# The right forms' loads and stores on ScalarE's queue: a change in layer 0's second MLP pair

## The chip, the cores and the metric

The kernel runs on one core of a Trainium2 chip. The metric is the device time of one execution in microseconds (us). Three executions of the kernel before took 1452.15, 1454.65 and 1456.01 us; their median is 1454.65.

The core has engines with instruction streams of their own: TensorE (PE in the profile) multiplies matrices, VectorE (DVE) does elementwise work on two operands, ScalarE (ACT) casts, copies and evaluates functions, GpSimd (POOL) does a little work here, and SyncE (SP) only starts transfers (DMAs). Each engine takes its instructions in the order in which the program gives them; between engines, semaphores hold an instruction until what it needs is there.

## What is computed

Two layers, each a Fourier mixing (matrix products with DFT matrices along the sequence and along the hidden dimension), then a block with a spatial shift and an MLP. Cut to what matters:

```python
for layer in range(2):
    n = layernorm(x)
    a, b = n @ hid_re.T, n @ hid_im.T
    x = x + seq_re @ a - seq_im @ b
    z = layernorm(x)
    h = gelu(layernorm(z) @ w1)              # four column groups, shifted by +1, -1, +2, -2 rows
    z1 = z + shifted(h) @ w2
    x = x + z1 + gelu(layernorm(z1) @ w3) @ w4
```

The sequence has 2048 rows (S), the hidden dimension is 512 (D), the MLP's inner dimension 1376 (F). All is float32. TensorE takes a rounded kind of it, so each operand is split into a **high** part (ScalarE casts it) and a **low** part (VectorE subtracts the high part from the operand), and each product is three matmuls: high x high, high x low, low x high (`mm3`).

## The kernel before

Many products go through a form of fast matrix multiplication with seven products of half blocks instead of eight. For layer 1's Fourier mixing along the hidden dimension, the seven **right forms** of the hidden DFT matrices are made once, split into high and low, and kept in DRAM (`hsd`, seven tensors of two halves each, L65). They are made in layer 0, beside the second MLP pair, and that is where the change is.

**The MLP by pairs.** The rows are treated in two pairs of chunks (`for pair in range(n_pairs)`, L1258). In layer 0's second pair (`next_too`), after a first stretch of two w4 parts, five **passes** run (`for p in range(NF // 2)`). A pass has seven products of six matmuls each (`prod`) in the order b1, b6, b5, b2, b7, b4, b3, each into one of four PSUM banks taken in turn, and between b7 and b4 two w4 parts of twelve matmuls each (one in pass 0). ScalarE copies the first product (`copy u`), VectorE adds the others to it and to one another (seven additions a pass, into the `rest` tiles; L567 is the helper `add`), and ScalarE applies gelu and casts. A product can start only when the last addition that reads its bank's former content is done; the bank of b5 is read by two additions, the later of which is behind b7. A w4 load (`w4_load`, L943, 512 KB) is issued on SP behind every w4 part, a w3 load (`w3_load`, L958, 1792 KB) at the end of passes 0 to 2.

**The points.** Work that belongs to something else is given out in small steps: `bg` is a list of steps, and `one()` (L1116) runs the next. There are 26 points in the pair: points 0 and 1 in the first stretch, then in each pass one behind b5 (A), one behind gelu of b7's sum (B), one behind each w4 part (C, D), and one at the end (E). Pass 0 has points 2 to 5, pass 1 points 6 to 10, pass 2 points 11 to 15, pass 3 points 16 to 20, pass 4 points 21 to 25. The list's own steps (`early`, L1133) prepare layer 1: for each of four row groups statistics, normalisation, sums, casts and lows, one step each.

**The right forms beside them.** They are made in four quarters, and each part is put around one of the list's steps. A quarter loads two row blocks, m (imaginary) and r (real), each 256 KB; their left and right halves are b11, b12, b21, b22. Four **sums** on VectorE make three sums in three buffers (numbered 0, 1, 2) and the last one over b12. Then four **parts** cast and split seven forms into these three buffers by turns: a cast of each on ScalarE ahead of the step, its low on VectorE behind the step, and, right behind the low, a store of 256 KB on SP (`highs_`, `lows_`, L1219 to 1232). So a quarter takes five points: the sums at the first, then the parts with 3, 2, 1 and 1 forms. Quarter n has points 5n to 5n + 4; the next quarter's m and r are loaded on SP behind its last two points, and the next sums come one point later. Quarter 0's m and r are loaded in pair 0 (`then[9]`, L1376).

On SP everything is in one row: the stores of the forms, which wait for their lows; m and r; the w4 and w3 loads. Buffers 1 and 2 lie where later gelu's output of the fifth pass is kept (`hx`, L126).

Of the kernel before, what the change touches and what calls it, by code (L numbers as in the profile page):

```python
# [8 lines left out]
F32 = mybir.dt.float32  # L9
F32R = mybir.dt.float32r  # L10
AF = mybir.ActivationFunctionType
ALU = mybir.AluOpType
# [33 lines left out]
def spectral_mlp_kernel(ctx: ExitStack, tc: tile.TileContext, x, ws, hs, w1, w2, w34, out):  # L46
    nc = tc.nc
# [17 lines left out]
    hsd = [[dram.tile([P, 2, CH], F32, name=f"hsd{i}{j}") for j in range(2)] for i in range(7)]  # L65
# [15 lines left out]
    base = -(-nc.sbuf_base // 32) * 32  # L81
# [76 lines left out]
    def piece(src, a=0, b=2):  # L158
        pieces.append((src, a, b))
        return len(pieces) - 1  # L160
# [25 lines left out]
    for layer in range(LAYERS):  # L186
        for c in range(NC):
# [15 lines left out]
            for k in range(NP):  # L203
# [4 lines left out]
                p = piece(ws[c, k][:, 2:4])  # L208
# [18 lines left out]
    raws, slots, sums, place = {}, {}, {}, {}  # L227
# [299 lines left out]
    def low(tf):  # L527
        nc.vector.tensor_tensor(tf[0][:, :, 1], tf[1][:, :, 1], tf[0][:, :, 0].bitcast(F32), op=ALU.subtract)
# [37 lines left out]
    def add(o, a, b, op=ALU.add):  # L566
        nc.vector.tensor_tensor(o, a, b, op=op)  # L567
# [290 lines left out]
    def by_pairs(layer, zs, xin, dst):  # L858
# [51 lines left out]
        def sum_of(*names):  # L910
            return lambda: b_sum(*names)
# [41 lines left out]
        def w3_load(n):  # L953
            if n >= n_pairs * (NF // 2):
                return
            if layer or n >= NF // 2:
                i = (n + (last_of(layer) and n >= NF // 2)) % 2
                nc.sync.dma_start(w3b[i].bitcast(F32), w3d[n % (NF // 2)])  # L958
                return
            nc.sync.dma_start(staged.rearrange("p f k w -> p f (k w)"), w34[2 * n : 2 * n + 2, :, 0].rearrange("f p w -> p f w"))  # L960
# [116 lines left out]
        steps = [(shifted, 0, g) for g in GORDER]  # L1077
# [32 lines left out]
        bg, prep = [], {}  # L1110
# [9 lines left out]
        def do_all(*fs_):  # L1120
            return lambda: [f() for f in fs_]
# [22 lines left out]
        def next_steps():  # L1144

            steps = (
                ((ay_lows, 2), (ay_sums, 3), (ay_highs, 3), (more, 1)),
                ((ay_lows, 3),),
                ((xp_stats, 4), (keep_rows, 8)),
                ((xp_stats, 5), (more, 2)),  # L1150
                ((xp_norm, 4),),
                ((xp_sums, 4), (xp_highs, 4), (more, 3)),
                ((ax_lows, 4), (xp_norm, 5)),
                ((ay_lows, 4), (ax_sums, 5), (ax_highs, 5), (more, 4)),
                ((ax_lows, 5), (keep_rows, 10)),
                ((ahead, 1), (more, len(pieces))),
                ((ahead, 1),),
                ((ahead, 1),),
                (),
            )  # L1160
            return [[do(*s)] for s in steps]
# [30 lines left out]
            ]  # L1192

        def hs_forms():
            steps = []
            for n in range(4):
                d, v = n // 2, slice(n % 2, n % 2 + 1)
                m, r = (at(f"hs{i}{n}", RAWS + (1 + i) * CH, 1, CH, dtype=F32) for i in range(2))
                fp = [both(f"hp{i}{n}", word, 1, 2, DH) for i, word in enumerate((RAWS + 3 * CH, STG, STG + CH))]
                steps += hs_quarter(m, r, fp, [(t[d][:, v], hs[(1, d)][:, v], hs[(0, d)][:, v]) for t in hsd])  # L1200
            return steps

        def hs_quarter(m, r, fp, places):
            b11, b12, b21, b22 = (t[:, :, v] for t in (m, r) for v in (left, right))
            raw = [tf[:, :, 1] for _, tf in fp]

            def load_m():
                nc.sync.dma_start(m, places[0][1])

            def load_r():  # L1210
                nc.sync.dma_start(r, places[0][2])

            def sums():
                add(raw[1], b12, b11, ALU.subtract)
                add(raw[2], b22, b12, ALU.subtract)
                add(raw[0], b22, raw[1], ALU.subtract)
                add(b12, raw[0], b21, ALU.subtract)

            def outs(*which):  # L1219
                which = [(i, n, raw[i] if src is None else src) for i, n, src in which]  # L1220

                def highs_():
                    for i, _, src in which:
                        act(fp[i][0][:, :, 0], src)

                def lows_():
                    for i, n, src in which:
                        t = fp[i][0]
                        nc.vector.tensor_tensor(t[:, :, 1], src, t[:, :, 0].bitcast(F32), op=ALU.subtract)
                        nc.sync.dma_start(places[n][0].rearrange("p i (l w) -> p i l w", l=2), t.bitcast(F32))  # L1230

                return highs_, lows_

            nothing = lambda: None
            parts = [
                (nothing, sums),
                outs((1, 3, None), (2, 4, None), (0, 2, None)),
                outs((1, 0, b11), (2, 1, b12)),
                outs((0, 6, b21)),
                outs((1, 5, b22)),  # L1240
            ]
            return [(load_m, load_r), *parts]

        def next_block(c, half, to):
            return lambda: b_in(c, half, to)
# [12 lines left out]
        for pair in range(n_pairs):  # L1258
# [10 lines left out]
            if next_too:  # L1269
                hcs[8:] = [hx[:, 0], hx[:, 1], rest[0]]  # L1270
                bg += [lows("t4"), *early]
                for n in range(4):
                    parts = work[6 * n + 1 : 6 * n + 6]
                    for i, (before, behind) in enumerate(parts):
                        more_ = []
                        if n < 3 and i > 2:
                            more_.append(work[6 * n + 6][i - 3])
                        bg[5 * n + i] = do_all(before, bg[5 * n + i], behind, *more_)
            elif pair:
                bg.append(lows("t4"))  # L1280
            sets = [rest[4:8], rest[4:8]]
# [6 lines left out]
            for i, names in enumerate((("11", "21"), ("12", "22"))):  # L1288
                for d in range(KD):
                    b = blk[names[d // 2]]  # L1290
                    v = slice(d * P, (d + 1) * P)
# [29 lines left out]
            for p in range(NF // 2):  # L1321
                prep = {} if kept else w_prep(p)
                u, v, x, y = sets[p % 2]
                w = w3b[(5 * pair + p) % 2]
# [48 lines left out]
            then = [[] for _ in range(NF + 2)]  # L1373
            if pair == 0:
                work = hs_forms()
                then[9] = [*work[0]]  # L1376
                next_blocks((3, 1, "22"))
                then[1] = [lambda: w3_load(NF // 2)]
                then[2] = [lambda: rows(xs[0], dst, 0, 2, False)]
                then[3] = [lambda: rows(xs[1], dst, 2, 2, False)]  # L1380
                then[4] = [sum_of("t1", "12", "11"), sum_of("t2", "22", "t1")]
                then[5] = [sum_of("t3", "22", "12"), sum_of("t4", "21", "t2"), highs("11", "21")]
                names = "11", "21", "12", "22", "t2", "t1", "t3", "t4"
                for i in range(6):
                    then[6 + i] += [lows(names[i]), highs(names[i + 2])]
                then[8] += [lambda: w3_load(NF // 2 + 1)]
                then[12] = [lows("t3")]
            if next_too:
                then = next_steps()
            if next_too:  # L1390
# [497 lines left out]
    for layer in range(LAYERS):  # L1888
# [4 lines left out]
        for c in range(NC):  # L1893
            if layer == 0 and c == 0:
# [22 lines left out]
                def second_low(i):  # L1917
# [165 lines left out]
        for i, (ri, dp) in enumerate(HORDER):  # L2083
# [76 lines left out]
```

## Time and profile before

| | us |
|---|---|
| median of three executions | 1454.65 |
| profiled execution | 1454.98 |
| its span in the profile | 1452.9 |
| TensorE busy | 1420.9 |
| VectorE busy | 1204.9 |
| ScalarE busy | 731.8 |
| the stretch with the five passes, in the span | 615.6 to 698.3 |

A row of the timeline gives the start, the duration, the engine, the line, the operation, the output and inputs, their sizes, and in brackets how long the engine stood idle ahead of it and what ended that. Names are those of the program with numbers left out: `hp` is a buffer of the forms, `hs` is m or r (and, in `hs<-in_hs`, their load), `hsd<-hp` a store, `rest` the tiles of the additions, `psa` to `psd` PSUM banks, `w3b` and `w4r` the weights. A name such as `hp11f` is buffer 1 of quarter 1. L1208 is the load of m, L1211 that of r, L1224 a cast, L1229 a low, L1230 a store. SPq is SP's queue: the time in it is that in which an issue occupies the queue. Rows that follow one another on VectorE and ScalarE overlap a little (0.42 us long, 0.34 us from start to start), so work that follows on is counted from start to start.

### The profile page before, as it was taken

What the parts mean: (1) busy time and instruction counts of PE and PEld (TensorE: products, weight loads), DVE (VectorE), ACT (ScalarE), POOL (GpSimd) and SP (SyncE); (2) the same over time, 40 slices, a digit from 0 to 9 for tenths busy, and PEclk for the clock granted to TensorE, in tenths of its full rate; (3) what the DMA queues carried; (4) which work ended last, traced back from release to release, by engine and by line L of the source; (5) the groups of instructions that cost most, each with busy time, mean ns of one, the idle gap of its engine ahead of it and who ended that gap; (6) DMA issues with size and microseconds to landing.
All of it is one profiled execution on the core that took longest, in us unless ns stands there. A gap on an engine that the chain in (4) does not pass through costs nothing.

```text
span 1452.9 us, 18506 instructions
## 1 busy us (share of the span) xinstructions
PE 1420.9 (98%) x6681; PEld 1188.4 (82%) x6681; DVE 1204.9 (83%) x1725; ACT 731.8 (50%) x1020; POOL 76.6 (5%) x105
## 2 busy tenths in 40 slices
PE   9999999999999999998999989989989999999999
PEld 7888888888888888876888878878878888899887
DVE  7986998989978897667799878879879797897676
ACT  5663554445566654344555443444445666444342
POOL 2100000000002000000000000000000011000000
PEclk9999999999999999999999999999999999999999
DMA  7867657568645758877655577576687537586864
GB/s 247 274 204 234 200 173 261 173 200 296 226 133 161 268 214 282 329 251 263 232 173 190 203 256 225 187 269 222 207 294 240 173 102 275 165 250 217 320 205 163
DMA packets 145628, 325.24 MB, mean 224 GB/s; under 512 B 10624, under 2 KB 61568, under 8 KB 142848
## 3 DMA queue, kind: packets, MB, share of 16 engines
q1 hardware_dynamic: 145536, 324.05, 66.9%
q8 instruction: 53, 0.87, 0.2%
q14 instruction: 39, 0.32, 0.1%
HBM read 262.41 MB, written 61.60 MB: 223 GB/s over the span
## 4 chain that ended last, share of the span: by engine, by line
PE 83%; DVE 9%; DMA 4%; ACT 2%; issue 2%; SPq 0%; DVEq 0%; ACTq 0%
PE psd L343 8%; PE psd L345 8%; PE psd L344 8%; PE psa L343 7%; PE psa L344 7%; PE psa L345 7%; PE psb L344 6%; PE psb L343 6%; PE psb L345 6%; PE psc L344 6%; PE psc L345 6%; PE psc L343 6%; DVE ring L300 1%; DVE rest L567 1%; DMA raw<-in_ws 1%
## 5 line engine op out<-in xcount | busy, mean ns | idle before, releaser
L300 DVE TENSOR_TENSOR ring<-raw,ring 128x1024 fp32r<-128x1024 f32 x102 | 124.2, 1220 | 19.0 <-ACT ring L279 18.7
L279 ACT CAST ring<-raw 128x1024 fp32r<-128x1024 f32 x103 | 107.8, 1051 | 56.3 <-PE psd L345 25.6
L383 POOL TENSOR_TENSOR rs<-ve,mhalf 128x4 f32<-128x4 f32 x16 | 25.0, 1562 | 746.1 <-DVE nm L382 746.1
L343 PE MATMUL psd<-ring,ay 128*128 128x512 f32 x126 | 50.1, 398 | 7.8 <-DVE tmp L567 7.8
L300 DVE TENSOR_TENSOR ring<-ring1f,ring 128x512 fp32r<-128x512 f32 (+1 forms) x56 | 53.3, 952 | 2.9 <-ACT ring L282 2.9
L286 ACT CAST ring<-ring0f 128x1024 fp32r<-128x1024 f32 x28 | 29.5, 1053 | 50.5 <-DVE ring0f L285 50.2
L286 ACT CAST ring<-ring2f 128x1024 fp32r<-128x1024 f32 x28 | 29.6, 1056 | 48.8 <-DVE ring2f L285 48.8
L343 PE MATMUL psd<-rawr,hf 128*128 128x256 f32 x168 | 47.7, 284 | 5.8 <-issue 4.8
L343 PE MATMUL psc<-ring,ay 128*128 128x512 f32 x128 | 50.2, 392 | 2.0 <-ACT rr11f L608 1.7
L300 DVE TENSOR_TENSOR ring<-ring3f,ring 128x1024 fp32r<-128x1024 f32 (+1 forms) x50 | 49.3, 986 | 3.0 <-ACT ring L282 2.6
L362 POOL TENSOR_TENSOR rs<-ve,mhalf 128x2 f32<-128x2 f32 (+2 forms) x33 | 29.2, 886 | 426.6 <-DVE nb L361 407.6
L391 ACT ACTIVATE tmp<-xs,nb,rs 128x512 f32<-128x512 f32 x56 | 43.3, 810 | 15.8 <-POOL nb L363 12.6
L344 PE MATMUL psb<-ring,ay 128*128 128x512 f32 x128 | 50.3, 393 | 0.8 <-DVE ring L300 0.8
L343 PE MATMUL psb<-ring,ay 128*128 128x512 f32 x128 | 50.5, 394 | 0.0
L345 PE MATMUL psb<-ring,ay 128*128 128x512 f32 x128 | 50.1, 391 | 0.0
L345 PE MATMUL psd<-ring,ay 128*128 128x512 f32 x126 | 49.9, 396 | 0.0
L344 PE MATMUL psc<-ring,ay 128*128 128x512 f32 x128 | 49.8, 389 | 0.0
L345 PE MATMUL psc<-ring,ay 128*128 128x512 f32 x128 | 49.8, 389 | 0.0
L344 PE MATMUL psd<-ring,ay 128*128 128x512 f32 x126 | 49.8, 395 | 0.0
L344 PE MATMUL psa<-ring,ay 128*128 128x512 f32 x126 | 49.0, 389 | 0.0
L343 PE MATMUL psa<-ring,ay 128*128 128x512 f32 x126 | 49.0, 389 | 0.0
L345 PE MATMUL psa<-ring,ay 128*128 128x512 f32 x126 | 49.0, 389 | 0.0
(896 smaller groups left out, 4757.8 us busy)
## 6 DMA issues: line engine op xcount, KB each, us to landing
raw<-in_ws SPq DMA_DIRECT2D x183, 512.0 KB, 5.2
w4r<-w4d SPq DMA_DIRECT2D x44, 512.0 KB, 5.3
rawr<-hsd SPq DMA_DIRECT2D x42, 512.0 KB, 4.8
w3b<-w3d SPq DMA_DIRECT2D x10, 1792.0 KB, 9.3
raw<-in_hs SPq DMA_DIRECT2D x32, 512.0 KB, 4.0
w3d<-w3b SPq DMA_DIRECT2D x5, 1792.0 KB, 7.0
hsd<-hp SPq DMA_DIRECT2D x28, 256.0 KB, 2.4
x1d<-tmp SPq DMA_DIRECT2D x12, 512.0 KB, 7.4
```

The costliest lines, as they stand in the source:

```text
L279: nc.scalar.copy(dest[:, a:b, 0], r[0][:, a:b])
L286: nc.scalar.copy(dest[:, :, 0], lo)
L300: nc.vector.tensor_tensor(lo, src, hi.bitcast(F32), op=ALU.subtract)
L343: nc.tensor.matmul(o, lh, rh, start=first, stop=False, skip_group_check=more)
L344: nc.tensor.matmul(o, lh, rl, start=False, stop=False, skip_group_check=more)
L345: nc.tensor.matmul(o, ll, rh, start=False, stop=last, skip_group_check=more)
L362: nc.gpsimd.tensor_tensor(rs[:, :n], ve[:, :n], mhalf[:, 0, :n], op=ALU.pow)
L383: nc.gpsimd.tensor_tensor(rs, ve, mhalf[:, :, :2], op=ALU.pow)
L391: nc.scalar.activation(o, s, AF.Identity, bias=mr[2], scale=mr[1])
L567: nc.vector.tensor_tensor(o, a, b, op=op)
```

## The change

The stores, and the loads of quarters 1 to 3, go through ScalarE's queue (`nc.scalar.dma_start`) instead of SP's. A store is no longer issued behind its low, but at the next point, ahead of everything else there. Quarter 0's loads stay on SP.

A quarter takes six points (`base = 6 * n - 1`): the sums at `base`, then five parts at the next five points with 2, 1, 2, 1 and 1 forms. Stores come at `base + 2` to `base + 6`. The m load is two points ahead of the sums, the r load in the sums' own point, ahead of the step; at that point first the last store of the quarter before, then the r load, then the step, then the sums. Quarter 0's sums move into pair 0 (`then[12]`), behind its last w4 part and ahead of the drain of its second chunk. The sums are reordered so that each buffer is overwritten in another turn: the forms are the same.

```diff
-            def load_m():
-                nc.sync.dma_start(m, places[0][1])
-
-            def load_r():
-                nc.sync.dma_start(r, places[0][2])
+            def load_m(queue=nc.scalar):
+                queue.dma_start(m, places[0][1])
+
+            def load_r(queue=nc.scalar):
+                queue.dma_start(r, places[0][2])
 
             def sums():
-                add(raw[1], b12, b11, ALU.subtract)
                 add(raw[2], b22, b12, ALU.subtract)
-                add(raw[0], b22, raw[1], ALU.subtract)
-                add(b12, raw[0], b21, ALU.subtract)
+                add(raw[1], raw[2], b11, ALU.add)
+                add(raw[0], b12, b11, ALU.subtract)
+                add(b12, raw[1], b21, ALU.subtract)
...
-                def lows_():
+                def rest_of():
                     for i, n, src in which:
                         t = fp[i][0]
                         nc.vector.tensor_tensor(t[:, :, 1], src, t[:, :, 0].bitcast(F32), op=ALU.subtract)
-                        nc.sync.dma_start(places[n][0].rearrange("p i (l w) -> p i l w", l=2), t.bitcast(F32))
+
+                def store():
+                    for i, n, _ in which:
+                        nc.scalar.dma_start(places[n][0].rearrange("p i (l w) -> p i l w", l=2), fp[i][0].bitcast(F32))
...
             parts = [
-                (nothing, sums),
-                outs((1, 3, None), (2, 4, None), (0, 2, None)),
-                outs((1, 0, b11), (2, 1, b12)),
-                outs((0, 6, b21)),
-                outs((1, 5, b22)),
+                outs((0, 3, None), (2, 4, None)),
+                outs((1, 2, None)),
+                outs((0, 0, b11), (2, 1, b12)),
+                outs((1, 6, b21)),
+                outs((0, 5, b22)),
             ]
...
+                ahead_, behind_ = [[] for _ in bg], [[] for _ in bg]
                 for n in range(4):
-                    parts = work[6 * n + 1 : 6 * n + 6]
-                    for i, (before, behind) in enumerate(parts):
-                        more_ = []
-                        if n < 3 and i > 2:
-                            more_.append(work[6 * n + 6][i - 3])
-                        bg[5 * n + i] = do_all(before, bg[5 * n + i], behind, *more_)
+                    load_m, load_r, sums_, parts = work[n]
+                    base = 6 * n - 1
+                    if n:
+                        ahead_[base - 2].append(load_m)
+                        ahead_[base].append(load_r)
+                        behind_[base].append(sums_)
+                    for i, (cast, rest_of, store) in enumerate(parts):
+                        ahead_[base + 1 + i].append(cast)
+                        behind_[base + 1 + i].append(rest_of)
+                        ahead_[base + 2 + i].insert(0, store)
+                bg[:] = [do_all(*a, f, *b) for a, f, b in zip(ahead_, bg, behind_)]
...
-                then[9] = [*work[0]]
+                then[9] = [lambda: (work[0][0](nc.sync), work[0][1](nc.sync))]
...
-                then[12] = [lows("t3")]
+                then[12] = [lows("t3"), lambda: work[0][2]()]
```

More of the change, by code (lines that the diff above doesn't have):

```diff
@@ L1194, in hs_forms @@
         def hs_forms():
-            steps = []
+            groups = []
             for n in range(4):
@@ L1199, in hs_forms @@
                 fp = [both(f"hp{i}{n}", word, 1, 2, DH) for i, word in enumerate((RAWS + 3 * CH, STG, STG + CH))]
-                steps += hs_quarter(m, r, fp, [(t[d][:, v], hs[(1, d)][:, v], hs[(0, d)][:, v]) for t in hsd])
-            return steps
+                groups.append(hs_quarter(m, r, fp, [(t[d][:, v], hs[(1, d)][:, v], hs[(0, d)][:, v]) for t in hsd]))
+            return groups
         def hs_quarter(m, r, fp, places):
@@ L1205, in hs_quarter, with cast @@
             raw = [tf[:, :, 1] for _, tf in fp]
-            def load_m():
-                nc.sync.dma_start(m, places[0][1])
-            def load_r():
-                nc.sync.dma_start(r, places[0][2])
+            def load_m(queue=nc.scalar):
+                queue.dma_start(m, places[0][1])
+            def load_r(queue=nc.scalar):
+                queue.dma_start(r, places[0][2])
             def sums():
-                add(raw[1], b12, b11, ALU.subtract)
                 add(raw[2], b22, b12, ALU.subtract)
-                add(raw[0], b22, raw[1], ALU.subtract)
-                add(b12, raw[0], b21, ALU.subtract)
+                add(raw[1], raw[2], b11, ALU.add)
+                add(raw[0], b12, b11, ALU.subtract)
+                add(b12, raw[1], b21, ALU.subtract)
             def outs(*which):
                 which = [(i, n, raw[i] if src is None else src) for i, n, src in which]
-                def highs_():
+                def cast():
                     for i, _, src in which:
                         act(fp[i][0][:, :, 0], src)
-                def lows_():
+                def rest_of():
                     for i, n, src in which:
@@ L1229, in lows_ @@
                         nc.vector.tensor_tensor(t[:, :, 1], src, t[:, :, 0].bitcast(F32), op=ALU.subtract)
-                        nc.sync.dma_start(places[n][0].rearrange("p i (l w) -> p i l w", l=2), t.bitcast(F32))
-                return highs_, lows_
-            nothing = lambda: None
+                def store():
+                    for i, n, _ in which:
+                        nc.scalar.dma_start(places[n][0].rearrange("p i (l w) -> p i l w", l=2), fp[i][0].bitcast(F32))
+                return cast, rest_of, store
             parts = [
-                (nothing, sums),
-                outs((1, 3, None), (2, 4, None), (0, 2, None)),
-                outs((1, 0, b11), (2, 1, b12)),
-                outs((0, 6, b21)),
-                outs((1, 5, b22)),
+                outs((0, 3, None), (2, 4, None)),
[3 more added lines that the diff above has]
+                outs((0, 5, b22)),
             ]
-            return [(load_m, load_r), *parts]
+            return load_m, load_r, sums, parts
         def next_block(c, half, to):
```

## The prediction

> **What bounds the kernel now.** I read the page first, then the busy time by stretches of 10 us, then who waits for whom while layer 0's second MLP pair runs its five passes, then the chain of waits and the queues one by one.
>
> ```profile
> span 1452.9 us, 18506 instructions
> PE 1420.9 (98%) x6681; PEld 1188.4 (82%) x6681; DVE 1204.9 (83%) x1725; ACT 731.8 (50%) x1020; POOL 76.6 (5%) x105
> ```
> ```profile
> 650.00:660.00 10.00, 8.42 (x38) 6.63 (x36) 6.05 (x17) 1.02 (x3) 1.00 (x2) 1.00 0.82 329
> 660.00:670.00 10.00, 7.88 (x33) 6.22 (x34) 7.21 (x14) 7.57 (x14) 0.00 (x0) 1.00 0.74 232
> ...
> 680.00:690.00 10.00, 9.67 (x36) 7.85 (x37) 7.88 (x16) 7.18 (x14) 0.00 (x0) 0.83 0.63 209
> ```
> ```profile
> PE psa L343 <- DVE rest L567: 4.3, 3, 3.1
> PE psd L343 <- DVE rest L567: 3.3, 2, 2.7
> ```
>
> TensorE sets the time: 98% busy over the whole. In the stretches (columns: length, then PE, PEld, DVE, ACT, POOL busy, the granted clock, DMA) it falls short here, and in the whole stage it waits for nothing but VectorE, 4.3 + 3.3 = 7.6 us, always for an addition that reads a PSUM bank. How much the stage loses in all comes from TensorE's own order in time.
>
> ```profile
> 615.57 0.39 PE L343 MATMUL psa<-b,w3b 128*128 128x512 f32 x1
> ...
> 643.72 0.40 PE L343 MATMUL psd<-b,w3b 128*128 128x512 f32 x1
> ...
> 661.48 0.50 PE L343 MATMUL psa<-b,w3b 128*128 128x512 f32 x1 [3.05 <-DVE rest L567]
> ...
> 662.97 0.39 PE L343 MATMUL psa<-b,w3b 128*128 128x512 f32 x1
> ...
> 680.33 0.79 PE L343 MATMUL psd<-b,w3b 128*128 128x512 f32 x1 [2.67 <-DVE rest L567]
> 680.93 0.63 PE L344 MATMUL psd<-b,w3b 128*128 128x512 f32 x1
> ...
> 690.18 0.39 PE L343 MATMUL psc<-w4r,h 128*128 128x512 f32 x1
> ...
> 698.34 0.39 PE L343 MATMUL psc<-w4r,h 128*128 128x512 f32 x1
> ```
>
> Between 690.18 and 698.34 stand 36 matmuls (two w4 parts of 12, two products of 6): 0.2267 us from start to start. The five passes hold 54 + 4 x 66 = 318 matmuls, which would take 72.1 us. They take 698.34 - 615.57 = 82.8 us. **10.7 us** are lost; what the 7.6 us of waits don't hold is slow restarting (after the 2.67 us wait 0.60 and 0.43 us from start to start, and a granted clock of 0.83 in that row). Why is VectorE late?
>
> ```profile
> 634.74 0.43 DVE L567 TENSOR_TENSOR hp11f<-hs 128x256 f32<-128x256 f32 x1 [2.38 <-DMA hsd<-hp]
> ...
> 635.88 0.42 DVE L567 TENSOR_TENSOR hs<-hp01f,hs 128x256 f32<-128x256 f32 x1
> ...
> 643.16 0.76 DVE L1229 TENSOR_TENSOR hp<-hs,hp 128x256 fp32r<-128x256 f32 x2 [0.99 <-ACT hp L1224]
> ...
> 653.82 0.43 DVE L567 TENSOR_TENSOR hp12f<-hs 128x256 f32<-128x256 f32 x1 [3.72 <-DMA hsd<-hp]
> ...
> 672.60 0.42 DVE L567 TENSOR_TENSOR hp13f<-hs 128x256 f32<-128x256 f32 x1 [3.25 <-DMA hsd<-hp]
> ```
> ```profile
> 646.66 0.42 SPq L1208 DMA_DIRECT2D hs<-in_hs  x1
> 647.18 0.38 SPq L943 DMA_DIRECT2D w4r<-w4d  x1
> 647.65 0.39 SPq L1230 DMA_DIRECT2D hsd<-hp  x1
> 648.09 0.47 SPq L1211 DMA_DIRECT2D hs<-in_hs  x1
> 648.66 0.44 SPq L958 DMA_DIRECT2D w3b<-w3d  x1
> ```
> ```profile
> 629.65 4.66 DMA hsd<-hp
> ...
> 648.09 6.22 DMA hs<-in_hs
> ```
>
> At each of the three later quarters VectorE stands still ahead of the first sum: 2.38, 3.72 and 3.25 us. That sum overwrites a buffer whose store was issued on SP just before (647.65), between a w4 load, the r load (648.09) and a w3 load; in the chain such a store lands after 4.66 us, the r load after 6.22. VectorE's lateness reaches TensorE some products later.
>
> **The change part by part.** *Work taken away:* none. Sums, casts, lows, 28 stores and 8 loads are as many as before; the sums only change their order and which buffer takes which. What moves is when, and on which queue.
>
> ```profile
> L1230 SPq DMA_DIRECT2D hsd<-hp x28: 319/357/411, 619.7 to 685.3; - x28
> ...
> DMA to landing us min/median/max: 2.0/2.4/6.0
> ```
> ```profile
> L1208 SPq DMA_DIRECT2D hs<-in_hs x4: 423/428/440, 599.8 to 665.9; - x4
> ...
> DMA to landing us min/median/max: 3.3/5.4/6.3
> ```
> ```profile
> SPq L1230 <- DVE hp L1229: 57.5, 17, 9.4
> ```
> ```profile
> 608.29 0.69 DVE L1108 TENSOR_TENSOR xs<-psc,xs 128x512 f32<-128x512 f32 x1 [3.12 <-PE psc L345]
> ```
>
> *SP* loses 28 stores and 6 loads, and with them 57.5 us of standing behind lows. TensorE shows no wait for a DMA in this stage, so its w4 and w3 loads coming earlier are worth nothing by themselves.
>
> *The first quarter's sums* move ahead of pair 0's drain. Four sums take 1.6 us (634.74 to 636.30). VectorE idles 3.12 us ahead of the drain at 608.29, and both loads were issued by 600.8, so with the longest landing of 6.3 us the sums run from 607.1 at the latest and delay the drain by at most 0.4 us; the drained banks are written first at 622.4. I take 0; if that cover failed, 1.6 us.
>
> *Six points a quarter* instead of five: VectorE has 6.05 + 7.21 = 13.3 us of work in the 20 us from 650, so 12.8 in the pass of 19.25 us from 643.72 to 662.97. The forms are 4 sums and 7 lows of about 0.34, 3.7 us; a sixth less in each pass leaves 12.2. A pass of 66 matmuls is 15.0 us.
>
> ```profile
> DVE hp L1229 <- ACT hp L1224: 4.5, 5, 1.4
> ...
> DVE h L766 <- ACT h L776: 3.0, 4, 0.8
> ...
> DVE ax2f L422 <- ACT xs L391: 0.4, 1, 0.4
> ```
>
> VectorE's waits for ScalarE's casts, (4.5 + 3.0) / 4 + 0.4 = 2.3 us a pass, stay. So it has 15.0 - 12.2 - 2.3 = 0.5 us to spare in each pass.
>
> *34 issues on ScalarE's queue.* No row of before shows one there. Lower bound 0, if they are hidden entirely; above, SP's row, 0.36 a store and 0.43 a load. I take SP's: 34 over 24 points and five points a pass are 7, 2.8 us beside ScalarE's 1.02 + 7.57 = 8.6, 11.4 of 15.0. What is queued behind a waiting store are the next cast, and then gelu and the copies that free PSUM banks.
>
> *The three sums that waited* now wait for the r load, issued ahead in the same point, right behind the store of the quarter's last part. Both can go out when the last low is done, if ScalarE's queue gets there in time. What the landing is on a queue of its own is unknown: 3.3 at least by the row, 6.3 at most; I take 4.0, nearer the least, because only its own store of 256 KB is ahead of it and no load of w4.
>
> ```profile
> 636.82 1.28 DVE L357 BATCH_NORM_STATS2 st<-xs 128x6 f32<-128x512 f32 x2
> ...
> 668.40 0.95 DVE L448 TENSOR_TENSOR ax<-ax2f,ax 128x768 fp32r<-128x768 f32 x1
> ```
>
> The durations are those from start to start in such rows (an addition 0.60, the statistics 1.75 with the small aggregations behind them, sums and lows 0.34).
>
> - Quarter 1 (point 5): pass 0's fifth product ends 30 matmuls after 615.57, at 622.4; from there two additions 1.2, ax sums 0.95, a low, low1 0.61, the last low and the ends between them give 626.1; store 0.4; the r load lands at 626.5 + 4.0 = 630.5. VectorE itself gets there at 630.0 (low2 behind gelu and cast, then ax lows 0.87). Wait 0.5. The addition that frees the bank came 5.9 us after the sums and comes 5.5 after them now, at 637.6; TensorE wants the bank 114 matmuls after 615.57, at 641.4. Nothing reaches it.
> - Quarter 2 (point 11): from the last low, VectorE has one addition and the statistics, 2.35 us; the load needs 0.36 + 4.0. Wait 2.0, of which 0.5 is to spare: 1.5 reaches TensorE.
> - Quarter 3 (point 17): four additions, 2.4 us. Wait 2.0, of which 1.5 reaches TensorE.
>
> Loss 3.0 instead of 10.7: a gain of 7.7 us. The profiled execution took 1454.98 us (its span of 1452.9 and 2.1 around it), 0.3 over the median of the three runs. 1454.98 - 7.7 = **1447.3 us**. With a landing of 3.3 both waits are 1.3, the loss 1.6, the time 1445.9; with 6.3 both are 4.3, the loss 7.6, the time 1451.9.
>
> That ScalarE's queue gets there in time means that a DMA doesn't stand behind a gelu that waits for VectorE. The Trainium skill, "Perfetto Trace Analysis", sections "DVE / Act Engine Instruction" and "DMA Instruction — HWDGE (DVE, Sync)", says that an ACT instruction is pushed into a wait queue and the sequencer goes on, while a DMA's own semaphore wait holds the sequencer. By the first half the sum above stands; by the second half all that follows a waiting store is held too. No run here shows either, since before has no DMA on that engine.
>
> **The rivals.**
>
> *A, the transfers stay as slow.* The second queue feeds the same transfers while w3 runs:
>
> ```profile
> w3b<-w3d SPq DMA_DIRECT2D x3, 1792.0 KB, 9.5
> ```
>
> With the old median of 5.4 us both waits are 3.4, the loss 5.8: 1454.98 - 4.9 = 1450.1 us. For it speak the DMA shares of 0.74 to 0.82 in the stretches; against it that the r load's worst landings had w4 bytes of the same queue ahead. The Trainium skill, "DMA: Bandwidth & Descriptors", section "Issuing engines are not separate DMA queues", speaks for this one: whoever issues, the transfers run on the same DMA engines and interleave, and only time to issue is saved.
>
> *B, ScalarE takes everything in order.* Then the r load follows gelu y in quarter 3: 0.6 + 0.36 + 4.0 = 5.0 of wait, 4.5 at TensorE, with quarter 2's 1.5 makes 6.0; and casts stand behind stores:
>
> ```profile
> ACT hp L1224 <- DMA hsd<-hp: 4.9, 5, 3.2
> ```
>
> Each buffer is now cast into one point after its last store was issued, three times a quarter, and about two of these points have no TensorE work between them. At 2.4 us of landing ScalarE needs 8.6 + 2.8 + 5/6 x 2 x 2.4 = 15.4 a pass, 0.4 over, 1.6 in four passes: loss 7.6, 1451.9 us.
>
> *C, slower: ScalarE becomes the bound through these casts.* The same, with stores that land as in the chain, 4.66: 8.6 + 2.8 + 7.8 = 19.2 a pass, 4.2 over TensorE's 15.0, 16.8 in four: 1454.98 - 10.7 + 16.8 = 1461.1 us. The break-even lies at a landing of 3.8 us on each exposed wait, slower by 0.3% at 4.4. The median of 2.4 speaks against it, the maximum of 6.0 and w3's 9.5 us in every pass for it.
>
> **How the numbers follow.** Forecast 0.50, A 0.17, B 0.13, C 0.20. A measurement of this kernel tells some 0.3%, 4.4 us, from no change, so faster is below 1450.3: the forecast and half of A, 0.58. Within: the other half of A and B, 0.21. Slower: C and a remainder, 0.21. The lower end is 1444, where all 10.7 us come back (1444.3). The upper end, 1459, holds A, B and C's milder part. The forecast's own range is 1446 to 1452.
>
> **What would show it.** Right: the three idle times ahead of the sums shrink to about 0.5, 2 and 2 us and are ended by the r load; TensorE's five passes take 75 us; SP shows no wait behind lows; the r load goes out right behind the last low. Wrong: idle times of 3 us and more before the sums (A), DMA issues right behind gelus (B), casts waiting 2 us and more for stores in most points and the copy that frees a bank late (C), or issues of over 0.5 us.

## The result, and the profile after

The changed kernel is slower, by 0.8%. Its median is 1464.88 us (1464.33 to 1469.52, four runs), that of the kernel before beside it 1454.14 (1452.15 to 1456.01, four runs); the ratio is 1.0081, with a 95% interval of 1.0056 to 1.0106. The forecast was 1447.3. The profiled execution took 1464.59 us. Its page:

```profile
span 1462.7 us, 18465 instructions
PE 1425.7 (97%) x6681; PEld 1192.7 (82%) x6681; DVE 1204.7 (82%) x1725; ACT 732.2 (50%) x1020; POOL 76.2 (5%) x105
```

VectorE and ScalarE do the same work as before (1204.9 and 731.8 us then). What grew is time in which TensorE waits. TensorE's own order in time, from the first matmul of the five passes to the first behind them, with the waits of over 0.5 us between:

```profile
614.61 0.39 PE L343 MATMUL psa<-b,w3b 128*128 128x512 f32 x1
...
643.83 0.50 PE L343 MATMUL psa<-b,w3b 128*128 128x512 f32 x1 [3.21 <-DVE rest L567]
...
650.43 0.50 PE L343 MATMUL psa<-bt,w3b 128*128 128x512 f32 x1 [0.58 <-DVE rest L567]
...
656.28 0.50 PE L343 MATMUL psd<-bt,w3b 128*128 128x512 f32 x1 [2.84 <-ACT rest L1335]
...
676.27 0.80 PE L343 MATMUL psd<-bt,w3b 128*128 128x512 f32 x1 [7.42 <-DVE rest L567]
...
706.61 0.39 PE L343 MATMUL psc<-w4r,h 128*128 128x512 f32 x1
```

The passes take 706.61 - 614.61 = 92.0 us where they took 82.8: against the 72.1 us of 318 matmuls the loss is **19.9 us instead of 10.7**, 9.2 more. The spans differ by 9.8. The rest: the passes begin 1.0 earlier, the stretch from their end to the first product with `rawr` is 2.4 longer (125.3 against 123.0), the stretch from there to the first product with `rr` is 0.9 shorter. The waits shown are 14.05 us; the other 5.9 us are slow restarting, 3.1 of them behind the longest wait, in the second of these rows and the start of the next (columns as in the prediction; the granted clock is the third figure from the end):

```profile
660.00:670.00 10.00, 8.85 (x39) 6.89 (x38) 7.25 (x15) 4.59 (x9) 0.00 (x0) 1.00 0.66 218
670.00:680.00 10.00, 3.73 (x9) 2.96 (x10) 4.06 (x8) 3.86 (x8) 0.00 (x0) 0.60 0.62 227
```

Who waits for whom in the stretch of the passes (sum, times, longest):

```profile
DVE hp L1229 <- ACT hp L1224: 17.5, 11, 5.4
ACT hp L1224 <- DMA hsd<-hp: 13.7, 5, 5.5
...
DVE hp21f L567 <- DMA hs<-in_hs: 4.6, 1, 4.6
...
DVE hp23f L567 <- DMA hs<-in_hs: 3.1, 1, 3.1
...
DVE hp22f L567 <- DMA hs<-in_hs: 1.5, 1, 1.5
```

There are two groups. VectorE waits 9.2 us for r loads ahead of the sums. And ScalarE's casts wait 13.7 us for stores (4.9 before), and VectorE's lows 17.5 us for these casts (4.5 before). Only one of TensorE's long waits comes from the first group. The sums of quarter 1 began at 636.57, 4.6 us late; VectorE has no gap from there to the addition that frees the bank for 643.83:

```profile
643.09 0.69 DVE L567 TENSOR_TENSOR rest<-rest,psa 128x512 f32<-128x512 f32 x1
```

The other two come from the second group. ScalarE's rows, then VectorE's:

```profile
655.34 0.41 ACT L1224 CAST hp<-hs 128x256 fp32r<-128x256 f32 x1 [3.12 <-DMA hsd<-hp]
655.65 0.58 ACT L1335 COPY rest<-psd 128x512 f32<-128x512 f32 x1
...
674.76 0.41 ACT L1224 CAST hp<-hs 128x256 fp32r<-128x256 f32 x1 [5.46 <-DMA hsd<-hp]
```
```profile
675.19 0.43 DVE L1229 TENSOR_TENSOR hp<-hs,hp 128x256 fp32r<-128x256 f32 x1 [5.43 <-ACT hp L1224]
675.54 0.68 DVE L567 TENSOR_TENSOR rest<-rest,psd 128x512 f32<-128x512 f32 x1
```

At 655.34 a cast has stood behind a store; the copy that frees `psd` is next on ScalarE, and TensorE starts at 656.28. At 674.76 another cast has; its low holds VectorE, the addition that frees `psd` is next there, and TensorE starts at 676.27 after 7.42 us. So 10.3 of the 14.05 us are casts behind stores. Why do the stores land so late? The chain of waits, which gives the start and the length of each transfer on it, beside SP's issues of w3's loads:

```profile
616.02 4.00 DMA hsd<-hp
...
623.46 4.09 DMA hsd<-hp
...
630.09 6.45 DMA hs<-in_hs
...
647.93 7.39 DMA hsd<-hp
656.60 3.49 DMA hs<-in_hs
...
666.28 8.45 DMA hsd<-hp
...
685.30 2.72 DMA hs<-in_hs
```
```profile
627.04 0.32 SPq L958 DMA_DIRECT2D w3b<-w3d  x1
```
```profile
646.05 0.32 SPq L958 DMA_DIRECT2D w3b<-w3d  x1
```
```profile
666.16 0.32 SPq L958 DMA_DIRECT2D w3b<-w3d  x1
```

The three long ones are those issued 0.1 to 3.1 us behind a w3 load. They land at 636.54, 655.32 and 674.73. The three w3 loads themselves take this long:

```profile
DMA to landing us min/median/max: 8.4/8.5/8.9
```

With 8.5, 8.9 and 8.4 us in their order they land at 635.5, 654.9 and 674.6, so each of the three long transfers lands 0.2 to 1.0 us behind the w3 load ahead of it, though that is on another queue. The others on the chain took 2.7 to 4.1. That they don't share the way evenly shows in what moved from 648 to 652, while the second w3 load was under way (packets and MB of each queue, then the issues of this stretch):

```profile
q1 hardware_dynamic: 92, 1.32, 98.5%
...
hsd<-hp ACTq DMA_DIRECT2D x3, 256.0 KB, 7.4
hs<-in_hs ACTq DMA_DIRECT2D x1, 256.0 KB, 7.7
```

ScalarE's queue is q10 on the page of this profile, and it has no row here: three stores and an m load were issued on it from 647.93 to 651.08, and not one of their packets ran in these 4 us. All 92 that ran are w3's (1.32 MB, 14 KB each). Behind the first w3 load none ran from 630.5 to 633 either. Behind the third, 75 packets of ScalarE's queue ran from 669 to 673 among 94 of w3's, with a tenth of the bytes, and the store issued at 666.28 still landed behind the load.

### The profile page after: what moved, and what is told of

Same layout as the page of the kernel before. It is cut to its first block, busy times and chain, and to the rows that moved or that the text cites. A ratio compares the mean times of both kernels' runs of the same rounds, so it can differ in the third digit from the quotient of the medians.

```text
span 1462.7 us, 18465 instructions
## 1 busy us (share of the span) xinstructions
PE 1425.7 (97%) x6681; PEld 1192.7 (82%) x6681; DVE 1204.7 (82%) x1725; ACT 732.2 (50%) x1020; POOL 76.2 (5%) x105
## 4 chain that ended last, share of the span: by engine, by line
PE 81%; DVE 9%; DMA 5%; ACT 3%; issue 2%; SPq 0%; ACTq 0%; DVEq 0%; POOL 0%; POOLq 0%
PE psd L343 8%; PE psd L345 8%; PE psd L344 8%; PE psa L343 7%; PE psa L344 7%; PE psa L345 7%; PE psb L344 6%; PE psb L345 6%; PE psb L343 6%; PE psc L344 6%; PE psc L343 6%; PE psc L345 6%; DMA hsd<-hp 2%; DVE ring L300 1%; DMA raw<-in_ws 1%
```

## The experiments

The length of the five passes, read as above, is the measure for all of them. It is that of one profiled execution of each kernel, and these lay up to 4.2 us from their kernel's median, so a difference of 1 to 2 us between two rows is not settled. Outside the passes the profiles differ by up to 8 us from one another: the stretch from `rawr` to `rr` alone took 300.2 to 306.4 us, and this follows no edit. Ratios are against the kernel before, measured beside each, with 95% intervals; times without a ratio are one run.

| kernel | passes, us | loss, us | median, us | ratio |
|---|---|---|---|---|
| before | 82.8 | 10.7 | 1454.14 | |
| after | 92.0 | 19.9 | 1464.88 | 1.0081 (1.0056 to 1.0106) |
| all on SP | 87.6 | 15.5 | 1460.80 | 1.0039 (1.0021 to 1.0057) |
| loads on SP, stores on ScalarE | 88.6 | 16.5 | 1463.17 | |
| stores on SP, loads on ScalarE | 90.6 | 18.5 | 1464.42 | |
| no w3 loads | 84.5 | 12.4 | 1458.79 | |
| w3 loads in seven pieces | 86.5 | 14.4 | 1463.14 | 1.0059 (1.0036 to 1.0083) |
| no stores | 78.0 | 5.9 | (1472.37) | |
| last store and r load early | 94.5 | 22.4 | 1464.48 | |
| other buffers for m and r | 87.7 | 15.6 | 1464.87 | 1.0069 (1.0054 to 1.0084) |
| the same, all on SP | 83.6 | 11.5 | 1458.34 | 1.0026 (1.0014 to 1.0037) |
| before, other buffers for m and r | 80.9 | 8.8 | 1452.55 | 0.9982 (0.9970 to 0.9994) |
| the same, and a fourth buffer | 74.2 | 2.1 | 1447.11 | 0.9940 (0.9922 to 0.9959) |

**The queue alone: all on SP.** The new order of points, with every load and store back on SP.

```diff
-            def load_m(queue=nc.scalar):
+            def load_m(queue=nc.sync):
-            def load_r(queue=nc.scalar):
+            def load_r(queue=nc.sync):
-                        nc.scalar.dma_start(places[n][0]...
+                        nc.sync.dma_start(places[n][0]...
```

> The changed schedule (six points a quarter, stores a point behind, r load in the sums' own point) with every store and load back on SP's queue. The five passes lost 10.7 us before and 19.9 after the change, against 318 matmuls back to back. Theory 'queue' (ScalarE's queue is what costs: its issues stand behind gelus and its transfers share with w3's): loss 5 to 12 us, time 1449 to 1456. Rival 'schedule' (the r load in the sums' own point and the casts one point behind a store cost, on whatever queue): loss 17 to 22 us, time 1461 to 1466.

Loss 15.5 us, between what the two theories gave: of the 9.2 that the change costs, the order of points costs 4.8 and the queue 4.4. The order brings the r load into the sums' own point. SP's issues, the chain and the waits of this kernel:

```profile
671.57 0.38 SPq L958 DMA_DIRECT2D w3b<-w3d  x1
672.04 0.91 SPq L1233 DMA_DIRECT2D hsd<-hp  x2
```
```profile
672.04 8.74 DMA hsd<-hp
```
```profile
DVE hp21f L567 <- DMA hs<-in_hs: 8.7, 1, 8.7
...
DVE hp22f L567 <- DMA hs<-in_hs: 6.3, 1, 6.3
```

A store right behind w3's load takes 8.74 us here too, on the same queue. What makes a transfer slow here is that it is issued just behind that load, whichever queue it is on.

**Half of the queue's part each.** Loads or stores alone back on SP (the first two pairs or the last pair of lines of the diff above).

> The changed kernel with the loads of m and r back on SP's queue and the stores left on ScalarE's. Theory: the r load then goes out without the gelu ahead of it, but in its own point still stands behind or beside w3's load, so the first sums still wait (5 to 9 us); the casts wait for stores that land with w3's load as in the changed kernel (12 to 15 us in sum); the passes' loss is 17 to 21 us, 1462 to 1467 us. Rival (the loads on ScalarE are what makes the queue's share of the loss): the casts' waits fall below 8 us and the loss to 15 to 16 us, as with everything on SP.

> The changed kernel with the 28 stores back on SP and only the six loads on ScalarE. If the stores on ScalarE's queue make the difference between the queues, the loss of the passes is about that of all on SP, 15.5 us, or less; if the loads do, it stays near 20 us.

The loads' return took the loss from 19.9 to 16.5, the stores' return to 18.5, both to 15.5: 3.4 and 1.4, together 4.8 against 4.4. By these single executions the loads are the larger half of the queue's part. With the loads on SP the casts waited 9.2 us in sum, between what the two theories gave, and the loss came near the rival's figure.

**Without w3's loads.** The three loads of w3 in layer 0's second pair are left out; its passes then multiply by what lies in the buffers.

```diff
-                if kept and not (pair == 0 and p >= NF // 2 - 2):
+                if kept and not next_too and not (pair == 0 and p >= NF // 2 - 2):
```

> The changed kernel without the three w3 loads (1792 KB each) of passes 0 to 2; passes 2 to 4 multiply by stale weights. Theory 'contention' (ScalarE's transfers land late because w3 moves at the same time): landings of stores and r loads fall to 2 to 3.5 us, waits of casts for stores from 13.7 to under 6 us, loss of the passes 5 to 9 us instead of 19.9. Rival 'order' (the issues are late on ScalarE, landing matters little): loss 15 us and more.

Loss 12.4, 7.5 less. Stores land in 4.7 us at most (8.4 in the changed kernel), and the longest wait of a cast falls from 5.5 to 3.2:

```profile
ACT hp L1224 <- DMA hsd<-hp: 8.3, 7, 3.2
```

So w3's loads account for most of the 9.2 us, but the loss stays above the 5 to 9 that the theory gave. The casts still wait 8.3 us for stores of at most 4.7, and the sums of quarter 3 wait 5.5 for an r load that was issued between two w4 loads.

**w3's loads in seven pieces.** As many bytes on SP, in transfers of 256 KB.

```diff
+                if layer == 0:
+                    for u in range(7):
+                        nc.sync.dma_start(w3b[i][:, :, u].bitcast(F32), w3d[n % (NF // 2)][:, :, u])
+                    return
                 nc.sync.dma_start(w3b[i].bitcast(F32), w3d[n % (NF // 2)])
```

> The changed kernel with every load of w3 in layer 0's second MLP pair issued on SP as seven transfers of 256 KB instead of one of 1792 KB. Theory (a transfer on ScalarE's queue stands behind the whole of w3's load because that load's pieces are handed out at once, 14 KB a partition): with seven short transfers the stores and the r load that meet w3 get their share, their landings fall from 4.3 to 6.5 us towards 2.5 to 4 us, the passes' loss falls from 19.9 to 13 to 16 us, the time to about 1458 to 1461 us. Rival (the 16 engines share by bytes outstanding whatever the cut, or all seven stand ahead anyway): the landings stay at 4 to 6.5 us and the loss at 18 to 21 us, 1463 to 1467 us. Should the cut make w3's own load slow, matmuls of the passes wait for w3b and the loss grows past 21 us.

Loss 14.4, 5.5 less, as the theory said. The expectation had the changed kernel's landings too short; by the chain they were 6.45, 7.39 and 8.45 us. Here the store on the chain that meets a w3 load lands in 5.24, none takes over 5.7, and casts wait 2.7 us at most. The waits, SP's issues and the chain:

```profile
ACT hp L1228 <- DMA hsd<-hp: 6.5, 7, 2.7
```
```profile
661.99 5.46 SPq L960 DMA_DIRECT2D w3b<-w3d  x7
```
```profile
664.56 5.24 DMA hsd<-hp
```

SP now spends 5.5 to 8.4 us to issue each seven, and w3's bytes are handed out over that time. So a 256 KB transfer beside one of 1792 KB waits for nearly all of it, and beside seven of 256 KB for less. The time bears this out only in part. The median is 1.7 us below the changed kernel's, within the rival's range, and the intervals overlap; the execution with this loss was the fastest of five, 4.2 us below their median. The landings, up to 5.7 us, did not fall to the theory's 2.5 to 4.

**Without the stores.** The 28 stores are left out, and `hsd` is filled in pair 0 by 14 transfers of other data. These lie ahead of the passes and lengthen the whole, so only the passes are compared.

```diff
-                        ahead_[base + 2 + i].insert(0, store)
...
+                for h in range(7):
+                    for j in range(2):
+                        nc.sync.dma_start(hsd[h][j], hs[(h % 2, j)])
```

> The changed kernel without the 28 stores of the forms; the forms' place in DRAM is filled with the DFT matrices by 14 transfers in pair 0, which the time holds too, so only the passes are compared. Theory 'casts behind stores' (the casts into a buffer whose store was issued a point earlier hold ScalarE, and VectorE behind it): loss of the passes 5 to 9 us instead of 19.9, what is left being the three r loads. Rival 'r load' (the sums' wait for the r load is the cost): loss 14 us and more.

Loss 5.9: with the casts' waits for stores gone, 14 of the 19.9 us are gone, although the sums still wait for r loads (the 28 issues and their bytes are gone too; the r loads did not get faster by it):

```profile
DVE hp21f L567 <- DMA hs<-in_hs: 5.6, 1, 5.6
...
DVE hp23f L567 <- DMA hs<-in_hs: 3.4, 1, 3.4
```

**Out from behind the gelus.** The quarter's last store and the next r load are issued right behind the last low, ahead of the next gelu.

```diff
-                        ahead_[base].append(load_r)
+                        behind_[base - 1] += [work[n - 1][3][4][2], load_r]
...
-                        ahead_[base + 2 + i].insert(0, store)
+                        if i < 4 or n == 3:
+                            ahead_[base + 2 + i].insert(0, store)
```

> The changed kernel with the store of each quarter's last part and the next r load right behind the last low, ahead of what follows on ScalarE, instead of a point later. Theory 'order' (on ScalarE a transfer's issue stands behind a gelu that still waits for VectorE): the r loads go out within 0.5 us of the last low (after the change 1.7, 0.2 and 3.2 us), the sums' waits shrink by 1.5 and 2 to 3 us for quarters 1 and 3. Rival 'landing' (the r load lands late whenever it goes out, because w3 moves): the waits shrink by less than 1 us each.

The r load of quarter 1 goes out at 627.35, 0.4 us behind the last low, instead of 630.09. But that is 0.3 us behind the issue of a w3 load, and it lands at 637.00 instead of 636.54. The chain and the waits:

```profile
627.35 9.65 DMA hs<-in_hs
```
```profile
ACT hp L1224 <- DMA hsd<-hp: 17.1, 8, 7.6
```

The sums of quarter 1 wait 6.3 us instead of 4.6, as the rival said. Those of quarters 2 and 3 wait 0.6 us between them instead of 4.6, as the theory said, yet the loss is 22.4: the casts wait 17.1 us for stores instead of 13.7. The delay behind gelus is real, but taking it away did not bring the loss down.

**r loads ahead of time.** m and r get other places by turns, so that r needn't wait for the quarter before, and both are loaded three points ahead of the sums.

```diff
-                m, r = (at(f"hs{i}{n}", RAWS + (1 + i) * CH, 1, CH, dtype=F32) for i in range(2))
+                at_ = (RAWS + CH, XS - 2 * CH, XS + 2 * CH, RAWS + CH)[n]
+                m, r = (at(f"hs{i}{n}", at_ + i * CH, 1, CH, dtype=F32) for i in range(2))
...
-                        ahead_[base - 2].append(load_m)
-                        ahead_[base].append(load_r)
+                        ahead_[base -3].append(load_m)
+                        ahead_[base -3].append(load_r)
```

> The changed kernel with m and r of quarters 1 and 2 in places of their own, both loads three points ahead of their sums, still on ScalarE's queue. Theory 'r load': the three waits of the sums (4.6, 1.5 and 3.1 us) fall to under 0.5 us each and the loss of the passes from 19.9 to about 11 us, time about 1455. Rival 'casts behind stores': the sums' waits go, but the casts' 13.7 us stay, loss 15 us and more, time over 1459.

No sum waits for an r load any more (two now wait 3.5 and 2.3 us for a store), and the loss is 15.6, 4.3 less. The casts wait no less than in the changed kernel, 15.4 us against 13.7. The whole time did not fall (1464.87): the stretch from `rawr` to `rr` took 306.4 us in this profile and 302.5 in the changed kernel's. Why is open.

**Both undone.** These places and times of m and r, with all on SP.

> The changed kernel with both parts undone that the runs so far price one by one: m and r in buffers of their own by turns, both loaded three points ahead of the sums (which took the passes' loss from 19.9 to 15.6), and every load and store of the making on SP's queue (which took it to 15.5). Theory (the two are separate causes, so that what they take away adds up): loss 9 to 13 us, casts' waits for stores 6 us or less, no wait of the sums above 2 us for an r load; outside the passes the runs differ by 3 us, so the time is 1452 to 1460 us. Rival (both runs took away the same thing, the traffic beside w3's load): loss 14 to 17 us, 1460 to 1465 us.

Loss 11.5, 8.4 less than 19.9; the two parts alone took off 4.3 and 4.4. They add up, as they would if they were separate. But the casts still wait 10.5 us for stores, where 6 or less was expected, and the sums 7.0. The one transfer on the chain is a store behind w3's load, again on its own queue:

```profile
668.18 9.71 DMA hsd<-hp
```

**The kernel before, with the same places of m and r**, loaded on SP two points ahead of the sums; then with a **fourth buffer** for a quarter's last form, too, so that the first sum overwrites a buffer stored two points earlier (the lines with `fp` and `outs`).

```diff
-                m, r = (at(f"hs{i}{n}", RAWS + (1 + i) * CH, 1, CH, dtype=F32) for i in range(2))
-                fp = [... enumerate((RAWS + 3 * CH, STG, STG + CH))]
+                at_ = (RAWS + CH, XS - 2 * CH, XS + 2 * CH, RAWS + CH)[n]
+                m, r = (at(f"hs{i}{n}", at_ + i * CH, 1, CH, dtype=F32) for i in range(2))
+                fp = [... enumerate((RAWS + 3 * CH, STG, STG + CH, (XS, RAWS + CH, XS + CH, STG)[n]))]
...
-                outs((1, 5, b22)),
+                outs((3, 5, b22)),
...
-                        if n < 3 and i > 2:
-                            more_.append(work[6 * n + 6][i - 3])
-                        bg[5 * n + i] = do_all(before, bg[5 * n + i], behind, *more_)
+                        if n < 3 and i == 3:
+                            more_ = work[6 * n + 6]
+                        bg[5 * n + i] = do_all(before, *more_, bg[5 * n + i], behind)
```

> The kernel before (everything on SP, five points a quarter) with m and r of quarters 1 and 2 in places of their own and both loads two points ahead of the sums. Theory 'stores behind the sums' (VectorE's three waits end with the store of the buffer that the first sum overwrites): the waits stay at 2 to 4 us and the loss of the passes at 8 to 11 us, time 1452 to 1456. Rival 'r load' (the r load is what the sums wait for): the waits vanish, loss under 4 us, time about 1447.

> The same as the run before it, and the last part of quarters 0 to 2 goes into a fourth buffer, so that no sum overwrites a buffer whose store was issued just before. If the store and the r load are all that holds VectorE in the kernel before, its three waits ahead of the sums (9.4 us) vanish, the loss of the passes falls from 10.7 to 1 to 4 us and the time to 1446 to 1449. If VectorE is short of time anyway, the loss stays over 6 us and the time over 1450.

With the places alone the sums still wait, 1.1, 3.7 and 3.7 us, for the store of the buffer that they overwrite, and the loss is 8.8. With the fourth buffer too it is 2.1, and the kernel takes 1447.11 us (1444.62 to 1448.90), less than both others. Its passes, its issues on SP around the first w3 load, and its waits:

```profile
614.60 0.39 PE L343 MATMUL psa<-b,w3b 128*128 128x512 f32 x1
...
688.84 0.39 PE L343 MATMUL psc<-w4r,h 128*128 128x512 f32 x1
```
```profile
628.56 0.37 SPq L1231 DMA_DIRECT2D hsd<-hp  x1
629.02 0.38 SPq L958 DMA_DIRECT2D w3b<-w3d  x1
635.59 5.40 SPq L1231 DMA_DIRECT2D hsd<-hp  x5
```
```profile
DVE hp02f L567 <- DMA hsd<-hp: 0.3, 1, 0.3
```

No wait of the sums is longer than that. Here the quarter's last store stands ahead of w3's load, and the next store comes 6.6 us behind it; in the two later passes 7.5 and 6.7. Five points a quarter against a pass's five points keep it so in each pass.

## Why the prediction was wrong, point by point

**The reading of before held.** The 10.7 us were the sums' waits: with these gone, the loss fell to 2.1 us and the time by 0.6%, close to the forecast's 7.7 us. But it was not the change that took them away.

**What the moves cost by themselves was priced well.** An issue on ScalarE takes 0.33 us for a store and 0.45 for a load (0.36 and 0.43 in the sum; seven a pass are 2.6 us by these prices, not 2.8). Quarter 0's sums lie ahead of the drain and cost TensorE nothing: its passes begin 1.0 us earlier than before. VectorE's rows:

```profile
606.05 0.42 DVE L567 TENSOR_TENSOR hp20f<-hs,hs 128x256 f32<-128x256 f32 x1 [1.85 <-DMA hs<-in_hs]
...
607.65 0.69 DVE L1108 TENSOR_TENSOR xs<-psc,xs 128x512 f32<-128x512 f32 x1
```

**The step that failed** is the one that left the casts' waits for stores out of the forecast's sum. They stood only in rivals B and C, and "the median of 2.4 speaks against it" set them aside. That landing belonged to the old order of points, five a quarter and five a pass, in which the next store was issued 8.5 to 9.6 us behind a w3 load (639.01 behind 630.55, for one). With six points a quarter the stores come to lie right behind w3's loads. In the new order the buffers are cast into one point after their stores were issued, and those on the chain landed in 4.00, 4.09, 7.39 and 8.45 us, all above the break-even of 3.8. The median of all 28 hardly moved, from 2.4 to 2.7 us; the casts waited for the slow ones, of which 12 took over 3.8 us where 4 had. It cost 10.3 us of TensorE's waits, and without stores 14 of the 19.9 us were gone.

**"Nearer the least, because only its own store ... is ahead of it and no load of w4"**, the 4.0 us for the r load, was mis-sized where a w3 load on the other queue stood ahead. The three took 6.45, 3.49 and 2.72; the sums waited 4.6, 1.5 and 3.1 us, where 0.5, 2.0 and 2.0 were forecast. Quarter 3 waited long although its load was quick, because it was issued late. (The row with 3.3, 5.4 and 6.3 us, from which the bounds were taken, is of the loads of m and r together; those of r alone had taken 4.9 us at least.) The price at TensorE lay elsewhere than forecast: 3.21 us at quarter 1, where "nothing reaches it", and none of the long waits comes from quarters 2 and 3.

**"ScalarE's queue gets there in time"** fell as well. The last low of quarter 2 is done at 682.14; its store and the r load of quarter 3 could have gone out then. ScalarE's rows:

```profile
684.93 0.63 ACT L763 ACTIVATE hc<-rest 128x512 f32<-128x512 f32 x1 [0.22 <-DVE rest L567]
684.94 0.33 ACTq L1233 DMA_DIRECT2D hsd<-hp  x1
685.30 0.45 ACTq L1211 DMA_DIRECT2D hs<-in_hs  x1
```

The gelu ahead of them waits for an addition on VectorE; the store goes out 0.01 us after the gelu has started, and the r load is 3.2 us behind the low (1.7 in quarter 1). The Trainium skill, "Perfetto Trace Analysis", section "DVE / Act Engine Instruction", says that the sequencer pushes an instruction into a wait queue and goes on; the trace shows no DMA that went out past a gelu that was still waiting. This is what B had said. The experiment with the early loads shows that this step was not what the change lost by: in quarter 1 the earlier load met w3, and in quarters 2 and 3 the waits went while the loss grew.

**Rival A** had the right mechanism for the transfers (a second queue feeds the same ones), and its price was too small, since it applied it to the r loads alone. **Rival C** had the place right (casts behind stores, then copies and additions late) and gave 1461.1. That it came near is in part luck: it left out the 6.0 us that B has for the r loads, with which it would give 1467.1. Its account was wrong, too: it made ScalarE too full, 19.2 us of 15.0 a pass, but ScalarE is busy for 3.9 to 4.6 of 10 us in the two stretches shown. It is not full; it stands still in the chain from low to store to cast to low.

## What to carry to other kernels

Price a moved transfer by what will be in flight when it is issued in the new order, the largest load above all; a landing measured in the old order holds only there. A second queue didn't keep a small transfer clear of a large one here, but an order did: small ones ahead of the large one, and the next not before most of it is through. Where a wait is for a buffer, first look for another buffer: here two places for m and r and a fourth for the forms gave what the new queue did not.

## What the runs showed of the hardware that was not expected

A 256 KB transfer issued while one of 1792 KB was under way ended behind it, although it was on another queue: in 4 us while the second w3 load was under way not one packet of the other queue ran, and behind the third these packets had a tenth of the bytes. In the changed kernel the eight that were issued 0.1 to 5.0 us behind a w3 load took 6.2 to 8.5 us; the quickest store took 2.0. With the large load in seven pieces no store took over 5.7.

Yet the two queues are not one row in the order of issue. With the stores on SP and the loads on ScalarE, a store was issued at 627.47 behind w3's load (627.05) and an r load at 627.78 on the other queue. They landed 10.6 and 9.8 us later, at 638.1 and 637.6: the one issued later came first, right behind w3's load, which took 10.3 (637.3).

The Trainium skill, "DMA: Bandwidth & Descriptors", section "Queues, rings and completion order", says that each DMA engine takes the queues by turns and drains a whole packet, typically 9 to 17 descriptors, before it switches. If the pieces of 14 KB are such descriptors, the w3 load has 128 of them, 8 for each of 16 engines: as an estimate from that figure, an engine's whole share is one packet, and the other queue's turn comes behind it. The trace agrees for the second w3 load; for the third it does so less, since some packets of ScalarE's queue ran among w3's. The runs don't show where a packet ends.

After TensorE had stood still for 7.42 us, its granted clock was 0.60 in that stretch of 10 us, and 1.00 in the one before it. The matmuls behind the wait followed one another at 0.43 us up to 682, where 0.23 is usual.
